# An FFT filter followed by a top-128 FFN on one core: first input in four pieces, inner tables in two, work moved between engines, and an order of issue written out

## The chip, the cores and the metric

The kernel runs on one core of a Trainium2 chip. The core has TensorE (PE in the rows; its weight loads are PEld), VectorE (DVE), ScalarE (ACT) and GpSimd (POOL), and SyncE (SP), which here only issues DMAs. Each engine takes its instructions in the order in which they were issued to it and waits where one of them needs a result that isn't there. The metric is the time of one execution on the device, in microseconds.

## The reference

```python
def _attn_ref(x, filt_r, filt_i):            # x: 8 x 3136 x 256
    X = np.fft.rfft(x, axis=1)
    F = (filt_r + 1j * filt_i)[None, :, :]
    return np.fft.irfft(X * F, n=x.shape[1], axis=1)

def _moe_ref(x, w_gate, w1, w2, capacity):   # capacity 128, w1: 256 x 1024
    scores = np.einsum('bsd,d->bs', x, w_gate)
    out = x.copy()
    for b in range(B):
        top_idx = np.argpartition(-scores[b], capacity)[:capacity]
        xe = x[b, top_idx]
        h = np.maximum(xe @ w1, 0.0)
        g = 1.0 / (1.0 + np.exp(-scores[b, top_idx]))
        out[b, top_idx] = x[b, top_idx] + g[:, None] * (h @ w2)
    return out
```

## The kernel before

The transform over 3136 = 98 x 32 points is done as two short transforms, both as matmuls with tables, for one batch of 8 at a time. A batch goes through these steps, which the code calls by short names:

- `load` brings a batch's half (128 of 256 channels) into the tile `X`, 113 partitions by 4096 values: one DMA for 112 partitions, one for the last row. There is one buffer for each half, so the next batch's half is loaded after the results of an earlier one were stored from it.
- `outer`, in 8 chunks of 32 channels: two `fold`s (sum and difference of the two halves of the points, into `xh` and in place), then four matmuls `amm` (tile `pa`). In the chunks of the list `UNF` ("plain") the folds are left out and `amm` is eight matmuls. `tout` turns the result with a transpose on DVE into `UU`. On the way back `tin` (a transpose into `t`), `ymm` (tile `py`) and `yout` (copy to `X`), and `store`. In the last two batches `imm`, `iout` and two `join`s on DVE or POOL (list `JOIN`) stand in their place.
- `inner`, in 7 groups of two table pairs (the last has one): `zmm` (tile `pz`, with the table `tf_sb`), then the products with the filter: `zout` (ACT copies `pz` to `q`) and `qmul` (POOL multiplies `q` by `fb_sb`), and `pmul` (DVE multiplies `pz` by `fa_sb` into `y`); then `vmm` (tile `pv`, with the table `ti_sb`) over both, and `vout` (ACT copies `pv` back to `UU`). The score of each row comes from `gate` (DVE, one per row group, tile `rj`), or for the pairs listed in `GPOOL` from `gmul` on POOL (tile `xl`, one buffer) and two sums `gsum` on ACT.
- `select` finds the top 128 of a batch by eight counting steps (`count` on ACT, `total` on PE, `over` on DVE or, where `SELM` is 0, on ACT) and some twenty small steps.
- `ffn` gathers the rows, runs the two layers and scatters. The first two batches go alone, then batches 2 to 4 and 5 to 6 together with each factor split in two, and the last batch alone at the end.

At the start there are 85 small matmuls without a purpose for the result (`warmup`), the first `load`, the tables `tf_sb` and `ti_sb` (half of the latter's columns is made on the chip by `turn_ti`: two copies on DVE, two negations on ACT), and the filter tables in four parts (`tables`), which have half of the partitions filled by copies (`spread`).

`z`, `a`, `v`, `y` and `m` are PSUM rings with one buffer each. All steps are put into a list with `op(when, engine, cost, function, reads, writes, ...)`. A planner in the kernel then takes them one by one, by estimated costs and by due times with a lead for each kind of step (the table `LEAN`), and the steps are issued in the order that comes out.

## Time and profile before

| | us |
|---|---|
| median of 3 runs | 492.16 |
| lowest and highest | 490.76, 493.91 |
| the profiled execution | 487.98 |
| its span on the core | 486.2 |
| PE, DVE, ACT, POOL busy | 441.9, 406.4, 288.3, 286.5 |

The span is from the first to the last instruction; 1.8 us of the execution lie around it. The profiled execution is 4.2 us shorter than the median of the other runs. A PE that is busy need not be at its peak, since matmuls overlap and their ends are modelled.

### The profile page before, as it was taken

To read this page: it belongs to the slowest core of one execution; us is meant where nothing else is said; L and a number is where in the kernel's file an instruction comes from. 1 tells how busy PE (TensorE), PEld (TensorE's weight loads), DVE (VectorE), ACT (ScalarE), POOL (GpSimd) and SP (SyncE) were. 2 spreads that over 40 slices of the span, in tenths; PEclk is the share of its full clock that TensorE was granted. 3 is DMA by queue.
4 is the path that set the end of the run, shared out by engine and by line. 5 is a ranking of instruction groups with operands and counts; after the bars stand their busy time and mean duration, and the time that the engine had idled before them with its cause. 6 is when DMAs were issued, how large, how long until landed. Compare 5 with 4: busy or idle time off the path is not lost.

```text
span 486.2 us, 10656 instructions
## 1 busy us (share of the span) xinstructions
PE 441.9 (91%) x4094; PEld 226.1 (47%) x4094; DVE 406.4 (84%) x1012; ACT 288.3 (59%) x603; POOL 286.5 (59%) x186
## 2 busy tenths in 40 slices
PE   9848979999899999899999999999998978798996
PEld 9424443334333444343444344345433546466995
DVE  0777979998999989997999999999997987885632
ACT  1056745667446855866577657655666878865320
POOL 0438965853538784857475538255743987966022
PEclk9978989999999999999999999999999989999999
DMA  8999715137186638462828382818340844534510
GB/s 218 279 244 251 200 45 154 36 93 196 32 242 176 170 95 216 127 182 56 224 58 236 97 229 66 241 44 218 72 134 4 253 135 101 150 72 117 122 45 32
DMA packets 59944, 68.87 MB, mean 142 GB/s; under 512 B 3174, under 2 KB 56422, under 8 KB 57830
## 3 DMA queue, kind: packets, MB, share of 16 engines
q1 hardware_dynamic: 59126, 66.10, 51.0%
q0 software_dynamic: 768, 2.10, 1.3%
q8 instruction: 32, 0.52, 0.5%
q14 instruction: 18, 0.15, 0.1%
HBM read 41.28 MB, written 26.91 MB: 140 GB/s over the span
## 4 chain that ended last, share of the span: by engine, by line
PE 34%; DVE 30%; DMA 19%; ACT 5%; issue 5%; POOL 4%; SPq 1%; POOLq 0%; DVEq 0%; ACTq 0%
PE py L447 8%; PE pv L301 7%; DMA X<-in_x_dram 6%; PE pa L381 6%; DVE UU L386 5%; DVE rj L317 5%; DMA ti_sb<-in_ti_dram 5%; DVE y L289 4%; DVE t L362 4%; DMA out_dram<-X 4%; PE pz L281 3%; DMA fb_sb<-in_fri_dram 3%; DVE X L370 2%; PE pa L410 2%; DVE xh L370 2%
## 5 line engine op out<-in xcount | busy, mean ns | idle before, releaser
L292 POOL TENSOR_TENSOR q<-q,fb_sb 128x1024 f32<-128x1024 f32 (+1 forms) x56 | 126.2, 2253 | 88.2 <-ACT q L285 75.1
L447 PE MATMUL py<-t,c_sb 128*98 128x512 f32 x192 | 104.8, 628 | 4.4 <-ACT X L450 3.9
L381 PE MATMUL pa<-X,c_sb 49*64 49x512 f32 x440 | 79.4, 601 | 2.8 <-DVE UU L386 1.2
L362 DVE STREAM_TRANSPOSE t<-UU 128x1024 f32<-128x1024 f32 x64 | 78.6, 1231 | 1.0 <-PE py L447 0.9
L301 PE MATMUL pv<-y,ti_sb 64*64 64x256 f32 x800 | 68.9, 397 | 8.0 <-DVE rj L317 7.8
L450 ACT COPY X<-py 98x512 f32<-98x512 f32 x96 | 55.7, 581 | 33.9 <-PE py L447 27.2
L317 DVE SCALAR_TENSOR_TENSOR rj<-pv,wg_sb 128x256 bf16<-128x256 f32 x150 | 62.9, 419 | 15.2 <-ACT UU L309 5.3
L386 DVE STREAM_TRANSPOSE UU<-pa 128x1024 f32<-128x1024 f32 x59 | 73.4, 1244 | 2.4 <-PE pa L381 1.5
L281 PE MATMUL pz<-UU,tf_sb 64*64 64x256 f32 x800 | 61.4, 406 | 9.8 <-DVE UU L386 5.0
L289 DVE TENSOR_TENSOR y<-pz,fa_sb 128x1024 f32<-128x1024 f32 (+1 forms) x56 | 63.5, 1134 | 7.5 <-ACT q L285 6.3
L285 ACT COPY q<-pz 128x1024 f32<-128x1024 f32 (+1 forms) x56 | 53.1, 948 | 24.4 <-PE pz L281 23.1
L301 PE MATMUL pv<-q,ti_sb 64*64 64x256 f32 x800 | 66.6, 385 | 0.0
L381 PE MATMUL pa<-xh,c_sb 49*64 49x512 f32 x168 | 50.4, 606 | 4.2 <-DVE UU L386 3.1
L370 POOL TENSOR_TENSOR xh<-X 113x512 f32<-113x512 f32 x27 | 37.4, 1385 | 27.2 <-DMA X<-in_x_dram 19.8
L281 PEld LDWEIGHTS pz<-UU,tf_sb 64*64 64x64 f32 x800 | 27.7, 135 | 49.8 <-issue 14.3
L301 PEld LDWEIGHTS pv<-y,ti_sb 64*64 64x64 f32 x800 | 29.7, 136 | 44.0 <-issue 10.0
L331 POOL TENSOR_TENSOR xl<-UU,wg_sb 128x512 f32<-128x512 f32 x25 | 34.7, 1387 | 15.8 <-ACT UU L311 11.6
L447 PEld LDWEIGHTS py<-t,c_sb 128*98 128x98 f32 x192 | 23.9, 163 | 36.3 <-ACT X L450 17.4
L588 ACT ACTIVATE junk<-R,nb 128x392 bf16<-128x392 f32 (+1 forms) x48 | 30.0, 625 | 18.1 <-DVE nb L607 16.8
L301 PEld LDWEIGHTS pv<-q,ti_sb 64*64 64x64 f32 x800 | 34.4, 137 | 12.9 <-issue 1.0
L309 ACT COPY UU<-pv 128x1024 f32<-128x1024 f32 x24 | 24.3, 1014 | 26.0 <-PE pv L301 25.9
L370 POOL TENSOR_TENSOR X<-X 113x512 f32<-113x512 f32 x23 | 30.6, 1332 | 13.0 <-DVE xh L370 11.9
(201 smaller groups left out, 696.8 us busy)
## 6 DMA issues: line engine op xcount, KB each, us to landing
X<-in_x_dram SPq DMA_DIRECT2D x16, 1792.0 KB
...
```

The lines of the kernel that those rows point to most:

```text
L281: nc.tensor.matmul(z[o, hi, e], lhsT=tf_sb[p, l], rhs=urow(b, l, 0, D)[p], start=True, stop=True)
L285: nc.scalar.copy(out=wide(q), in_=wide(h["z"]))
L289: nc.vector.tensor_tensor(out=wide(y), in0=wide(h["z"]), in1=filt(fa_sb), op=ALU.mult)
L292: nc.gpsimd.tensor_tensor(out=wide(h["q"]), in0=wide(h["q"]), in1=filt(fb_sb), op=ALU.mult)
L301: nc.tensor.matmul(v[o, j, c], lhsT=ti_at[p, k, 2 * i + e, hi], rhs=y[p, hi, c], start=k == 0, stop=k == 1)
L317: nc.vector.scalar_tensor_tensor(out=rj, in0=h["v"][:, k % 2, k // 2 * D:k // 2 * D + D], scalar=1.0, in1=wg_sb, op0=ALU.mult, op1=ALU.mul ...
L362: nc.vector.transpose(out=h["t"].rearrange("p d (l j) -> p d l j", j=2), in_=uchan(b_out, c))
L370: eng.tensor_tensor(out=(area(1) if k else h["f"])[:64 + NH], in0=area(0)[:64 + NH], in1=area(1)[:64 + NH], op=(ALU.add, ALU.subtract)[k])
L381: nc.tensor.matmul(ap[64 * k:64 * k + 64, g].rearrange("p (n d) -> p n d", d=DW), lhsT=todo[k][i][0][p], rhs=todo[k][i][1][p], start=i == ...
L386: nc.vector.transpose(out=uchan(b_in, c), in_=a.rearrange("p (l j) d -> p d l j", j=2))
L447: nc.tensor.matmul(yp[:N1], lhsT=cc["wi"], rhs=half(), start=True, stop=True)
L450: nc.scalar.copy(out=XO[:N1, hx, :, q * CW - hx * HD:(q + 1) * CW - hx * HD], in_=h["y", k][:N1])
```

## The change

1. The planner is gone. A list `ORDER` of 1803 numbers says in which order the steps of the list are issued. The numbers in `PLAN` are others too; the times among them no longer do anything but number the steps.
2. The first batch's input lies in DRAM by quarters of the channels, and is loaded in four pieces of 112 x 2048 values, each with its last row. In all loads that last row is now cut into 16 runs and goes ahead of the rest.
3. `tf_sb` is loaded in two pieces, one for the first two groups and one for the others, and so is `ti_sb`. The work of `turn_ti` is in eight pieces on DVE, ACT and POOL.
4. In the groups of `QDVE` (10 of 56; four of these are the short last group) the second product is made by DVE straight from `pz` (`qdir`), without ACT's copy and POOL's product.
5. `GPOOL` names pairs of either half of a group. 46 pairs go to POOL and ACT, 25 before.
6. There are 17 plain chunks, 20 before. Of the folds 17 are on DVE and 77 on POOL, 38 and 50 before. Where both joins of a chunk are on DVE (three chunks), they read the second operand from PSUM and one copy of ACT's goes.
7. `over` is on ACT in four batches, in two before; on DVE in four, in six before.

```diff
+ORDER = [
+    4, 6, 27, 3, 28, 29, 1, 30, 31, 18, 8, 19, 7, 9, 21, 23, 24, 11, 22, 25, 5, 32, 26, 16, 10, 12, 0, 35, 33, 13, 39,
...
+    QDVE=[[1, 2, 6], [0, 3, 6], [5, 6], [0], [6], [], [], []],
...
-    SELM=[1, 1, 0, 1, 1, 1, 0, 1],
+    SELM=[1, 0, 0, 1, 1, 1, 0, 0],
...
-    UNF=[[3, 4, 5, 7], [0, 3, 4, 6, 7], [0, 4], [0, 2], [], [0, 4], [0, 6, 7], [1, 7]],
-    GPOOL=[[0, 1, 2, 4, 5], [1, 2, 5], [2, 3, 4], [0, 2], [1, 3], [0, 2, 3], [1, 3, 4], [0, 1, 2, 3]],
+    UNF=[[0, 3, 4, 6, 7], [0, 1, 4, 7], [0], [0], [], [0, 4], [0, 6], [1, 7]],
+    GPOOL=[[0, 2, 7, 9, 10], [2, 3, 5, 8, 9, 10, 11], [0, 1, 4, 5, 8, 9, 10], [0, 2, 5, 6, 10, 11], [0, 1, 2, 3, 6,
+          9], [1, 3, 5, 6, 7, 9], [2, 3, 5, 7, 9], [1, 3, 5, 7]],
...
+            def qdir(h=h, wide=wide, filt=filt):
+                h["q"] = q = flt.tile([128, 2, 2 * D], F32, name="q", bufs=BUFS["q"])
+                nc.vector.tensor_tensor(out=wide(q), in0=wide(h["z"]), in1=filt(fb_sb), op=ALU.mult)
...
+            def fetch():
+                nc.sync.dma_start(out=to[112:113].rearrange("p (r e) -> p r e", r=16), in_=ends[h:h + 1])
+                nc.sync.dma_start(out=to[:112], in_=main[h])
...
+        def quarter(q):
+            to = x_flat[:, 2048 * q:2048 * q + 2048]
+            nc.sync.dma_start(out=to[112:113].rearrange("p (r e) -> p r e", r=16), in_=ends[q:q + 1])
+            nc.sync.dma_start(out=to[:112], in_=main[q])
...
+        to, of_ = (ti_sb[re, 1, at], ti_sb[im, 0, at]) if k else (ti_sb[im, 1, at], ti_sb[re, 0, at])
+        if eng == "act":
+            nc.scalar.activation(out=to, in_=of_, func=AF.Copy, scale=-1.0 if k else 1.0)
         else:
-            nc.scalar.activation(out=ti_sb[re, 1], in_=ti_sb[im, 0], func=AF.Copy, scale=-1.0)
+            (nc.vector if eng == "dve" else nc.gpsimd).tensor_scalar(out=to, in0=of_, scalar1=-1.0 if k else 1.0, scalar2=None, op0=ALU.mult)
...
     with tc.manual_schedule():
-        for n in order:
+        for n in ORDER:
             prog[n][4]()
```

In three places the move is shown by the instructions in a row. The first is SP's queue of DMAs at the start of the program, from the first input on; before (`in_x_dram` is the input, `in_fri_dram` the filter, `tf`, `ti` the inner tables):

```order
L475 DMA X<-in_x_dram 112x4096
L476 DMA X<-in_x_dram 1x4096
L991 DMA tf_sb<-in_tf_dram 128x1600
L1018 DMA ti_sb<-in_ti_dram 128x1664
L992 DMA wg_sb<-in_moe_w_gate_dram 128x256
L959 DMA UU<-in_cst_dram 128x16
L943 DMA fa_sb<-in_fri_dram 32x1024 x2
L943 DMA fb_sb<-in_fri_dram 32x1024 x2
```

and now, from the main part of the third quarter that is issued:

```order
L600 DMA X<-in_x_dram 112x2048
L1148 DMA ti_sb<-in_ti_dram 128x512
L1118 DMA tf_sb<-in_tf_dram 128x512
L1085 DMA UU<-in_cst_dram 128x16
L1120 DMA wg_sb<-in_moe_w_gate_dram 128x256
L599 DMA X<-in_x_dram 1x16x128
L600 DMA X<-in_x_dram 112x2048
L1069 DMA fa_sb<-in_fri_dram 32x1024 x2
L1069 DMA fb_sb<-in_fri_dram 32x1024 x2
```

The longer piece of `ti_sb` (128 x 1152) now stands ahead of all input, the short pieces of both tables behind three quarters of it, the fourth quarter behind these, and the longer piece of `tf_sb` behind the third part of the filter.

The second is DVE at the start, the end of the first batch's transposes into `UU` and what follows up to the first product; before (L977 are the copies of `turn_ti`, L950 those of `spread`, L962 fills a constant):

```order
L386 STREAM_TRANSPOSE UU<-pz 128x32x16x2
L977 COPY ti_sb<-ti_sb 32x1664
L386 STREAM_TRANSPOSE UU<-pv 128x32x16x2
L386 STREAM_TRANSPOSE UU<-pa 128x32x16x2
L977 COPY ti_sb<-ti_sb 32x1664
L386 STREAM_TRANSPOSE UU<-pz 128x32x16x2
L962 CAST cr_sb<-UU 128x16
L950 COPY fb_sb<-fb_sb 32x1024
L950 COPY fa_sb<-fa_sb 32x2048
L289 TENSOR_TENSOR y<-pz,fa_sb 128x1024 x2
```

and now:

```order
L488 STREAM_TRANSPOSE UU<-pv 128x32x16x2
L1076 COPY fb_sb<-fb_sb 32x1024
L488 STREAM_TRANSPOSE UU<-pa 128x32x16x2
L1106 TENSOR_SCALAR ti_sb<-ti_sb 32x512
L1088 CAST cr_sb<-UU 128x16
L1076 COPY fb_sb<-fb_sb 32x1024
L488 STREAM_TRANSPOSE UU<-pz 128x32x16x2
L1076 COPY fb_sb<-fb_sb 32x2048
L380 TENSOR_TENSOR y<-pz,fa_sb 128x1024 x2
L387 TENSOR_TENSOR q<-pz,fb_sb 128x1024
```

The long copies of `ti_sb` are no longer among the last transposes; two copies of `fb_sb` are there in their place, and the second group's second product follows the first products on DVE.

The third is POOL while the fifth batch's inner groups run (`q` are the products of `qmul`, `xl` those of `gmul`, `xh` and `X` the folds); before:

```order
L292 TENSOR_TENSOR q<-q,fb_sb 128x1024 x2
L331 TENSOR_TENSOR xl<-UU,wg_sb 128x512
L292 TENSOR_TENSOR q<-q,fb_sb 128x1024
L370 TENSOR_TENSOR xh<-X 113x512
L370 TENSOR_TENSOR X<-X 113x16x32
L292 TENSOR_TENSOR q<-q,fb_sb 128x1024
L370 TENSOR_TENSOR X<-X 113x16x32
L370 TENSOR_TENSOR xh<-X 113x512
L331 TENSOR_TENSOR xl<-UU,wg_sb 128x512
L292 TENSOR_TENSOR q<-q,fb_sb 128x1024
```

and now:

```order
L431 TENSOR_TENSOR xl<-UU,wg_sb 128x512
L472 TENSOR_TENSOR X<-X 113x16x32
L383 TENSOR_TENSOR q<-q,fb_sb 128x1024
L431 TENSOR_TENSOR xl<-UU,wg_sb 128x512
L383 TENSOR_TENSOR q<-q,fb_sb 128x1024 x2
L472 TENSOR_TENSOR X<-X 113x16x32
L472 TENSOR_TENSOR xh<-X 113x512
L431 TENSOR_TENSOR xl<-UU,wg_sb 128x512
L472 TENSOR_TENSOR xh<-X 113x512
L472 TENSOR_TENSOR X<-X 113x16x32
L383 TENSOR_TENSOR q<-q,fb_sb 128x1024
L431 TENSOR_TENSOR xl<-UU,wg_sb 128x512 x3
```

More folds and gate products stand between the products `q` on POOL, and three gate products stand in a row.

## Rows read from the trace of the kernel before

**Rows 1.** By stretch: length; PE, PEld, DVE, ACT, POOL busy; clock, DMA share, GB/s.
```profile
0.00:25.00 25.00, 22.65 (x247) 16.50 (x250) 9.55 (x9) 1.49 (x2) 5.99 (x10) 1.00 0.94 248
25.00:77.00 52.00, 38.49 (x442) 19.52 (x437) 42.95 (x62) 32.22 (x42) 36.76 (x21) 0.87 0.71 183
77.00:370.00 293.00, 280.94 (x2571) 118.03 (x2564) 273.32 (x712) 185.56 (x390) 172.83 (x102) 1.00 0.51 139
370.00:480.00 110.00, 98.30 (x840) 70.74 (x839) 80.12 (x229) 68.99 (x171) 69.99 (x52) 0.98 0.42 112
```
**Rows 2.** Whom PE waited for from 77 to 370 us: total, times, longest.
```profile
PE py L447 <- ACT X L450: 3.2, 6, 1.2
PE pa L381 <- DVE UU L386: 2.3, 5, 0.8
...
PE pv L301 <- DVE nd L593: 0.2, 1, 0.2
```
**Rows 3.** The start in order of time: start, duration, what.
```profile
1.21 0.41 SPq L475 DMA_DIRECT2D X<-in_x_dram  x1
...
12.54 0.69 DVE L370 TENSOR_TENSOR xh<-X 113x512 f32<-113x512 f32 x1 [12.54 <-DMA X<-in_x_dram]
...
20.67 1.28 POOL L370 TENSOR_TENSOR xh<-X 113x512 f32<-113x512 f32 x1 [1.93 <-DMA X<-in_x_dram]
...
25.88 1.02 DVE L977 COPY ti_sb<-ti_sb 32x1664 f32<-32x1664 f32 x1 [0.91 <-DMA ti_sb<-in_ti_dram]
...
29.30 1.02 DVE L977 COPY ti_sb<-ti_sb 32x1664 f32<-32x1664 f32 x1
...
31.66 1.99 PE L281 MATMUL pz<-UU,tf_sb 64*64 64x256 f32 x16 [4.06 <-DVE UU L386]
```
**Rows 4.** The chain that ended last: start, duration, what.
```profile
31.05 13.22 DMA fb_sb<-in_fri_dram
...
152.38 1.02 PE pa L381 x8
...
362.84 1.95 PE pa L381 x16
```
**Rows 5.** Groups of instructions of the gate: busy us, mean ns of one.
```profile
L317 DVE SCALAR_TENSOR_TENSOR rj<-pv,wg_sb 128x256 bf16<-128x256 f32 x150 | 62.9, 419 | 15.2 <-ACT UU L309 5.3 <-ACT UU L305 3.6 <-ACT UU L311 3.3
...
L331 POOL TENSOR_TENSOR xl<-UU,wg_sb 128x512 f32<-128x512 f32 x25 | 34.7, 1387 | 15.8 <-ACT UU L311 11.6 <-ACT Dt L506 2.2 <-ACT UU L309 2.0
...
L336 ACT ACTIVATE junk<-xl 128x256 bf16<-128x256 f32 x50 | 20.9, 418 | 6.5 <-POOL xl L331 5.3 <-ACT junk L588 0.4
...
L317 DVE DVE_READ_ACCUMULATOR rj<-pv,wg_sb 128x1 f32 x150 | 12.3, 82 | 0.0
...
L336 ACT ACTIVATION_READ_ACCUMULATOR junk<-xl 128x1 f32 x50 | 9.5, 189 | 0.0
```
**Rows 6.** Instructions of the folds' line: ns min/median/max, first and last start.
```profile
L370 POOL TENSOR_TENSOR xh<-X x27: 1251/1287/1762, 12.6 to 348.3; 113x512 f32<-113x512 f32 x27
...
L370 DVE TENSOR_TENSOR X<-X x21: 676/1209/2756, 13.3 to 356.2; 113x512 f32<-113x512 f32 x21
L370 DVE TENSOR_TENSOR xh<-X x17: 670/693/1985, 12.5 to 354.3; 113x512 f32<-113x512 f32 x17
```
**Rows 7.** Groups of the products with the filter, as in rows 5.
```profile
L292 POOL TENSOR_TENSOR q<-q,fb_sb 128x1024 f32<-128x1024 f32 x48 | 116.1, 2418 | 71.3 <-ACT q L285 58.2 <-ACT Dt L506 10.0 <-issue 2.0
...
L289 DVE TENSOR_TENSOR y<-pz,fa_sb 128x1024 f32<-128x1024 f32 x48 | 58.1, 1211 | 7.5 <-ACT q L285 6.3 <-issue 1.2
...
L285 ACT COPY q<-pz 128x1024 f32<-128x1024 f32 x48 | 48.5, 1010 | 23.8 <-PE pz L281 22.7 <-POOL q L292 0.6 <-POOL X L419 0.3
```
**Rows 8.** Groups of a counting step's end and of ACT's table load, as in rows 5.
```profile
L607 DVE TENSOR_SCALAR nb<-J,nd 128x1 f32<-128x1 f32 x48 | 10.3, 214 | 1.8
...
L612 ACT ACTIVATE nb<-J,nd 128x1 f32<-128x1 f32 x16 | 4.7, 295 | 0.5
...
L983 ACT ACT_TABLE_LOAD x1 | 1.3, 1283 | 0.7 <-PEq L1161 0.7
```

More of the change, by code (lines that the diff above doesn't have):

```diff
@@ L24 @@
 NROW = 13
+CUT = 2
 W7 = NROW * N2
@@ L320, in inner @@
             parts = sorted({part_of[2 * i + e] for e in range(m)})
-            op(t0, "pe", .49 * m + .04, zmm, [u for l in ls for u in row(b, l)] + ["tf"], new=Z, mode=1)
-            op(t0 + 1.0, "act", .09 + .43 * m, zout, [Z], [Z], new=Q)
+            op(t0, "pe", .49 * m + .04, zmm, [u for l in ls for u in row(b, l)] + [("tf", int(i >= CUT))], new=Z, mode=1)
+            direct = i in QDVE[b]
+            if not direct:
+                op(t0 + 1.0, "act", .09 + .43 * m, zout, [Z], [Z], new=Q)
@@ L323, in inner @@
             op(t0 + 1.0, "dve", .08 + .535 * m, pmul, [Z, *(("fa", k) for k in parts)], new=Y)
-            op(t0 + 2.0, "pool", .1 + 1.13 * m, qmul, [Q, *(("fb", k) for k in parts)], [Q])
-            op(t0 + 4.5, "pe", .88 * m + .02, vmm, [Y, Q, "ti"], new=V, mode=1)
+            if direct:
+                op(t0 + 1.1, "dve", .08 + .535 * m, qdir, [Z, *(("fb", k) for k in parts)], new=Q)
+            else:
+                op(t0 + 2.0, "pool", .1 + 1.13 * m, qmul, [Q, *(("fb", k) for k in parts)], [Q])
@@ L338, in inner @@
-            for ks in ([0, 1], [2, 3]):
-                ks = [k for k in ks if k < n]
-                if i in GPOOL[b] and ks == [2, 3]:
-                    G = ("xl", "g", b, i)
-                    op(t0 + 7.2, "pool", 1.3, gmul, [*(u for l in ls[2:] for u in row(b, l)), "wg"], new=G)
-                    op(t0 + 8.5, "act", .9, gsum, [G], [("u", b % 2, l, NDC) for l in ls[2:]])
+                    nc.scalar.activation(out=rk, in_=h["g", e][:, j], func=AF.Copy, accum_out=urow(b, ls[2 * e + j], D, DS))
@@ L344, in inner @@
+            for e in range(2):
+                ks = [k for k in (2 * e, 2 * e + 1) if k < n]
+                if 2 * i + e in GPOOL[b] and len(ks) == 2:
+                    G, us = ("xl", "g", b, i, e), ls[2 * e:2 * e + 2]
+                    op(t0 + 7.2, "pool", 1.3, lambda e=e, gmul=gmul: gmul(e), [*(u for l in us for u in row(b, l)), "wg"], new=G, tag="gmul")
+                    op(t0 + 8.5, "act", .9, lambda e=e, gsum=gsum: gsum(e), [G], [("u", b % 2, l, NDC) for l in us], tag="gsum")
                     continue
@@ L401, in outer @@
                 continue
-            if b_out >= B - INV:
+            if 2 * b_out + hx in INVH:
                 ir = IRING[c % len(IRING)]
                 PI_, E_ = (ir, "I", b_out, c), ("xh", "i", b_out, c)
+                on_dve = [2 * c + k in JOIN[b_out] for k in range(2)]
+                direct = all(on_dve)
                 def imm(h=h, ir=ir):
@@ L1065 @@
-    bufs = BUFS
-    full = {k: set(v) for k, v in uses.items()}
-    rings = {k: [[None, 0.0] for _ in range(n)] for k, n in bufs.items()}
-    users = [[] for _ in prog]
-    for n, d in enumerate(deps):
-        for m in d:
-            users[m].append(n)
-    left, ready, done = [len(d) for d in deps], [0.0] * len(prog), {}
-    free, can = {p[2]: 0.0 for p in prog}, {p[2]: [] for p in prog}
-    place_of, seen, pemode = {}, {}, 0
-    win, acc, cold = 0, 0.0, 0.0
-    free["sp"] = 1.0
-    for n, p in enumerate(prog):
-        if not left[n]:
-            can[p[2]].append(n)
```

214 lines of the change are left out of this document (80 added, 134 removed), and 85 rows, old and new, of the table ORDER.

## The prediction

> **What bounds the kernel now.** I read the busy times by stretch first, cut where the character of the work changes [rows 1]. From 0 to 25 us the DMA engines are busy for 0.94 of the time and move 248 GB/s: the start is a matter of bytes. From 25 to 77 us, up to the first transposes of the way back, PE is busy for 38.5 of 52 us, at a mean granted clock of 0.87, beside DVE with 43.0; the DMA engines are still at 0.71. From 77 to 370 us six batches pass in 293 us: PE is busy for 280.9 and DVE for 273.3, that is 96% and 93%. POOL (172.8) and ACT (185.6) have a third of that stretch free. The end, 370 to 480 us, has 11.7 us without PE and 29.9 without DVE.
>
> So PE is the bound of the middle, with DVE close behind, and what can be won there without less work on PE is its 12.1 us of idle time. Whom PE waited for there is in the waits [rows 2]: ACT's `yout` with 3.2 us is the first, then eleven rows with DVE as releaser, from 2.3 to 0.2 us, 7.1 us in all, and one of 0.8 for a DMA. This caps the worth of a faster DVE in the middle at 7 us, however much it is relieved.
>
> **The change part by part.** Work on PE: three plain chunks fewer. A plain `amm` took 1.95 us, one on folds 1.02 [rows 4], so 3 x 0.93 = 2.8 us less. PE has no cover for these, so I count them in full, -2.8.
>
> Work on DVE. The gate: 21 pairs, 42 instructions, leave it at 0.419 + 0.082 us each [rows 5]: -21.0. Folds: 14 in place and 7 into `xh` leave, at the medians 1.209 and 0.693 us [rows 6]: -21.8. `qdir`: six full products as long as `pmul`, 1.211 us [rows 7], and four half as large, at about half: +9.7. Three joins more at a fold's 0.693: +2.1. Two batches' eight steps of `over`, two instructions each, the second 0.214 us [rows 8], the first taken as equal: -6.8. Sum -38 us of 406.
>
> Work on POOL. 21 products for the gate at 1.387 [rows 5]: +29.1. 27 folds at 1.287 [rows 6]: +34.7. Six full products at 2.418 [rows 7] and four of half the size leave: -19.3. Three joins leave, at a fold's 1.287: -3.9. Sum +41 us of 286. On ACT: 42 sums at 0.418 + 0.189 [rows 5], +25.5; 16 `over` with two instructions of about 0.295 [rows 8], +9.4; ten copies, four of them half as large, at 1.010 [rows 7], -8.1. Sum +27 of 288. A second table load of 1.28 us (the one of before stood ahead of everything [rows 8]) now comes after the first `zout`. I cost it at nothing, since ACT's next necessary step there, the first `vout`, waits for the first `vmm`; without that cover it is 1.3 us.
>
> What the shift is worth in the middle. Nearly all of the DVE work leaves between 77 and 370 us, since batch 0 and batch 7 keep their number of gate pairs. DVE goes from 93% to about 80% there, POOL from 59% to about 73% and ACT from 63% to about 72%. PE's waits for DVE, 7.1 us, are bounded by none and all of them gone. I take 4 of them as gone, nearer to all, because a transpose or a gate on which PE waits was queued behind other DVE work in a 93% busy queue. Against it I set 1 us for ACT: `yout` is already the longest row of PE's waits [rows 2], and ACT gets sums and counting steps put between. Bounds of that: 0 and 3.2, its doubling. Net -3, with ends -7.1 and +3.2.
>
> Here a rule could speak against the change. The folds on DVE show what two engines do to each other: 0.670 us at best, a median of 1.209 and 2.756 at worst for the same shape [rows 6], and the products on POOL average 2.418. The Trainium skill says (Perfetto Trace Analysis, section Optimizing Scalar/DVE Operations) that DVE and GpSimd share an SBUF read port, so that moving work between the two might not help; by SBUF — State Buffer (section Who interferes with whom) it is DVE instructions with two SBUF inputs that collide. The rows agree as to the folds. But what moves away is folds, which collide, and gates, which read PSUM; the two-input instructions on DVE fall from 49 (38 folds, 11 joins) to 25. So by the rule, too, collisions on DVE would fall; no term rests on it.
>
> The start. Before, the first half of x landed at 12.5 us and the second at 20.7 [rows 3], 1.85 MB in 8.1 us. DVE then held two copies of `ti_sb` of 1.02 us among the last transposes, the first after 0.91 us of waiting for its DMA, and the first `zmm` of batch 0 ran at 31.66 us. Now 0.59 MB of `ti_sb` goes ahead of x, and 0.66 MB of tables, gate weights and constants between the third and the fourth quarter. The fourth quarter is therefore the later one: 1.25 MB more ahead of it, at 248 GB/s [rows 1] 5.0 us, on 20.7 gives 25.7. The last row of each load, a DMA of its own, no longer adds a whole row of 16 KB to one DMA engine beside seven on each; at an eighth of 8.1 us for each of two halves this gives back up to 2.0 us. So x is complete between 23.7 and 25.7 us instead of 20.7. Behind it stand two plain `amm` (the clock may be halved there as it was before), transposes and the two short copies of `fb_sb`: 24 + 2 x 1.95 + 1.2 + 0.7 gives the first `zmm` at about 30 us. That is 1.7 us gained where the bytes say a loss of 3 to 5, because `ti_sb` is then long finished. After that the chain of before waited for the third filter part up to 44.3 us [rows 4]. It is now ahead of the second half of the next x's rows, but the longer piece of `tf_sb`, which the third group needs, stands behind it; that lands at about the same 42 to 44 us. DVE's work from there to the end of batch 0 is unchanged within 1 us (two folds fewer, two products more). I take -2.5 for the stretch up to 77 us: 1.7 from the first `zmm` and something for the last two filter copies, which now come earlier. Ends: -6 (half of PE's 13.5 us of idle time goes) and +2 (the fourth quarter at 25.7 with a halved clock).
>
> The end. PE's idle 11.7 us after 370 us [rows 1] are spread over joins, gathers and the small steps of `select`. The split-weight matmuls now start among the last `imm`, so some of it fills; the last batch's `over` goes to ACT, which makes its counting longer by some 0.3 us in each of eight steps, but it stood some 10 us ahead of its use. I take -2, ends -5 and +2.
>
> Sum: -2.8 - 3 - 2.5 - 2 = -10.3 us. The profiled execution's 487.98 would become 477.7. It is 4.2 us under the median 492.16, so for a median I set the same difference there: **481.9, say 482**.
>
> **The rivals.** (A) The forecast, -10. (B) PE is the bound in any case. Consecutive matmuls into the same single buffer have to wait for its copy whoever is fast: `ymm`, then `yout`, then the next `ymm`, and the new order has such pairs as well. Then DVE's relief gives nothing, the end nothing, and only plain chunks and half of the start remain: -2.8 - 1.2 = -4, 488. For it: the first row of PE's waits is ACT. Against it: 7.1 us of DVE rows. (C) The balance frees more than the waits name, since a wait is put down to the last releaser alone, and the order is made for the new balance: -2.8 - 7.1 - 6 - 2, about -18, 474. For it: between a group's first and second matmuls the new order has more other PE work in batches 4 to 7. (D) Slower: POOL's queue. POOL gets 48 more instructions of about 1.35 us [rows 5, 6] (21 gate products and 27 folds), they stand between the products `q` for which `vmm` waits, and gate products in a row have to wait for two sums on ACT, 1.2 us, as `xl` has one buffer. If one in three of the 48 is ahead of a product that PE needs at once, 16 x 1.35 = 22 us come against 10 won: +11, 503. It decides from about one in six on (8 x 1.35 = 11 us). Against it: POOL sat idle for 71 us ahead of full products [rows 7], nearly all until ACT's copy was there, so it was usually early. (E) The fourth quarter decides the start: +2 there instead of -2.5, and with the rest as in A -6: 486.
>
> **How the numbers follow.** The measurement of this kernel can tell about 1% from no change (three runs of before lay 3.2 us apart). That puts the bounds at 487.2 and 497.1. A has 0.45, from 477 to 487; B 0.20; C 0.14; D 0.11; E 0.10. Faster by over 1%: nearly all of A (0.43), C, a third of B and two thirds of E, 0.70 in all, which I lower to 0.68. Within 1%: 0.20. Slower: D and the worst of E, 0.12. The range leaves out the far ends of C and most of D: 474 to 493.
>
> **What the profile of the changed kernel would show.** From about 75 us on six batches should pass in 286 us or so, with PE at 97% and DVE near 80%; PE's waits should name DVE for 3 us or less and ACT for more. The first `zmm` should stand at 30 us and DVE should reach the first transposes of the way back 2 us earlier. If POOL's products wait for nothing and PE's `vmm` waits for POOL, D was right. If DVE is at 80% and PE at 96% as before, B was. I would be wrong altogether if PE's busy time itself grew, by a halved clock in the middle.

## The result, and the profile after

The changed kernel takes **472.68 us** (median of 4 runs, 470.73 to 474.86), the kernel before 491.84 beside it: ratio 0.9607, interval 0.9553 to 0.9661. That is 19.2 us less where 10 were forecast, and 1.3 us under the lower end of the range. The profiled execution took 470.73 us with a span of 469.0 (before 487.98 and 486.2), so the two traces compared here differ by 17.2 us.

The first view is again the busy time by stretch. I cut where the same work stands as in [rows 1]: 76.3 us is just behind the first transpose of the way back, 356 just behind the seventh batch's `vs`, and 462.8 leaves the same 6.2 us at the end.

```profile
0.00:25.00 25.00, 22.89 (x242) 15.53 (x242) 9.30 (x9) 5.39 (x5) 7.05 (x11) 1.00 0.95 236
25.00:76.30 51.30, 39.66 (x471) 19.05 (x472) 42.00 (x63) 27.82 (x40) 36.99 (x23) 0.90 0.83 203
76.30:356.00 279.70, 270.80 (x2505) 115.94 (x2501) 245.47 (x591) 200.59 (x488) 209.22 (x137) 1.00 0.53 143
356.00:462.80 106.80, 99.33 (x857) 70.96 (x853) 77.58 (x211) 73.55 (x195) 66.13 (x50) 0.98 0.43 115
462.80:469.00 6.20, 1.46 (x11) 1.26 (x11) 0.48 (x1) 0.00 (x0) 0.96 (x1) 0.89 0.12 42
```

Against [rows 1] a stretch's time has two parts, PE busy and PE idle (length less the first figure). Idle: 15.9 to 13.8 us up to the first transposes, 12.1 to 8.9 in the middle, and 16.4 to 12.2 from there to the end (11.7 and 4.7 before, the last from the row 480 to 486.2: 1.52 busy of 6.20). That is -9.5 us. Busy: 441.90 to 434.15, -7.8 us. In the middle DVE went from 93% to 88%, POOL from 59% to 75%, ACT from 63% to 72%.

Whom PE waited for in the middle (total, times, longest), to be read against [rows 2]: ACT is still first, and of the eleven DVE rows (7.1 us) five remain with 4.4 us, 1.7 of them one wait for `vs`.

```profile
PE py L553 <- ACT X L556: 4.1, 7, 0.8
PE pm L627 <- DVE vs L622: 1.7, 1, 1.7
PE pa L483 <- DMA X<-in_x_dram: 1.0, 1, 1.0
PE pz L372 <- DVE q L387: 0.9, 1, 0.9
PE pa L483 <- DVE UU L488: 0.7, 2, 0.5
PE pm L723 <- DVE rows L832: 0.6, 1, 0.6
PE pz L372 <- DVE UU L488: 0.5, 1, 0.5
```

Over the whole span one wait is gone nearly altogether: `vmm` for the gate, which reads the one bank `pv` that the next `vmm` needs. The groups of the first half of `vmm`, before (L301) and after (L396); busy us and mean ns, then PE's idle time ahead of them:

```profile
L301 PE MATMUL pv<-y,ti_sb 64*64 64x256 f32 x800 | 68.9, 397 | 8.0 <-DVE rj L317 7.8 <-DVE nd L593 0.2
```
```profile
L396 PE MATMUL pv<-y,ti_sb 64*64 64x256 f32 x800 | 67.3, 385 | 2.1 <-ACT X L520 1.8 <-DVE rj L412 0.2
```

Of these 7.8 us only 1.3 lay in the middle. The kernel before had the others from 25 to 77 us and from 370 us on:

```profile
PE pv L301 <- DVE rj L317: 3.9, 4, 1.8
PE pv L301 <- DVE rj L317: 2.5, 2, 2.0
```

All rows of PE's waits that name DVE, added up over the whole span, come to 27.9 us before and 16.6 after. So 11.3 us of such waits went, and the middle has 2.7 of them.

The rows that answer to [rows 5 to 7], gate, folds and products, in two views of the changed kernel: groups, and the folds' line with ns min/median/max. A gate's instruction and a product cost what they did; the folds on DVE are fewer and no longer reach 2.76 us.

```profile
L412 DVE SCALAR_TENSOR_TENSOR rj<-pv,wg_sb 128x256 bf16<-128x256 f32 x108 | 45.3, 419 | 10.5 <-ACT UU L404 5.0 <-ACT UU L406 2.0 <-ACT UU L400 1.3
L431 POOL TENSOR_TENSOR xl<-UU,wg_sb 128x512 f32<-128x512 f32 x46 | 62.4, 1358 | 24.2 <-ACT junk L436 19.4 <-ACT UU L406 2.4 <-ACT UU L404 1.5
L383 POOL TENSOR_TENSOR q<-q,fb_sb 128x1024 f32<-128x1024 f32 x42 | 100.3, 2388 | 43.8 <-ACT q L376 43.5 <-DMA X<-in_x_dram 0.3
```
```profile
L472 POOL TENSOR_TENSOR xh<-X x37: 1253/1285/1716, 10.9 to 344.6; 113x512 f32<-113x512 f32 x37
L472 DVE TENSOR_TENSOR xh<-X x10: 649/764/1707, 58.3 to 296.1; 113x512 f32<-113x512 f32 x10
L472 DVE TENSOR_TENSOR X<-X x7: 651/725/1757, 12.2 to 263.6; 113x512 f32<-113x512 f32 x7
```

The start, answering to [rows 3]. The fourth quarter is there at 26.08 us and the last `amm` ends at 29.75, but the first `zmm` stands at 33.77, 2.1 us later than before:

```profile
29.35 0.42 DVE L1106 TENSOR_SCALAR ti_sb<-ti_sb 32x512 f32<-32x512 f32 x1
29.79 1.89 POOL L1076 COPY fa_sb<-fa_sb 32x2048 f32<-32x2048 f32 x1 [2.41 <-DVE ti_sb L1106]
29.80 1.91 DVE L1088 CAST cr_sb<-UU 128x16 fp32r<-128x16 f32 x1
...
32.46 1.25 DVE L488 STREAM_TRANSPOSE UU<-pz 128x1024 f32<-128x1024 f32 x1
...
33.77 1.66 PE L372 MATMUL pz<-UU,tf_sb 64*64 64x256 f32 x16 [4.02 <-DVE UU L488]
```

The list puts the CAST, the copy of `fb_sb` (0.69 us) and only then the last transpose, for which `zmm` waits. The CAST has 16 columns and took 1.91 us, from the start to the end of the copy on POOL beside it. In the kernel before it stood behind that transpose and took

```profile
31.64 0.18 DVE L962 CAST cr_sb<-UU 128x16 fp32r<-128x16 f32 x1
```

### The profile page after: what moved, and what is told of

Its sections match the earlier page's. It is cut to its first block, busy times and chain, and to the rows that moved or that the text cites. A ratio compares the mean times of both kernels' runs of the same rounds, so it can differ in the third digit from the quotient of the medians.

```text
span 469.0 us, 10671 instructions
## 1 busy us (share of the span) xinstructions
PE 434.1 (93%) x4070; PEld 222.8 (47%) x4070; DVE 374.8 (80%) x873; ACT 307.4 (66%) x725; POOL 320.4 (68%) x222
## 4 chain that ended last, share of the span: by engine, by line
PE 47%; DVE 15%; DMA 14%; POOL 9%; ACT 8%; issue 4%; SPq 1%; POOLq 0%; DVEq 0%; ACTq 0%
DMA X<-in_x_dram 12%; PE py L553 11%; PE pv L396 10%; PE pa L483 7%; PE pz L372 6%; DVE UU L488 3%; POOL q L383 3%; DVE y L380 2%; POOL xh L472 2%; POOL xl L431 2%; PE pa L514 2%; DVE t L462 2%; DMA out_dram<-X 2%; DVE rj L412 2%; POOL X L472 2%
## 5 line engine op out<-in xcount | busy, mean ns | idle before, releaser
L383 POOL TENSOR_TENSOR q<-q,fb_sb 128x1024 f32<-128x1024 f32 (+1 forms) x46 | 105.4, 2291 | 45.4 <-ACT q L376 45.1
L431 POOL TENSOR_TENSOR xl<-UU,wg_sb 128x512 f32<-128x512 f32 x46 | 62.4, 1358 | 24.2 <-ACT junk L436 19.4
L396 PE MATMUL pv<-y,ti_sb 64*64 64x256 f32 x800 | 67.3, 385 | 2.1 <-ACT X L520 1.8
L396 PE MATMUL pv<-q,ti_sb 64*64 64x256 f32 x800 | 65.3, 376 | 0.0
L472 POOL TENSOR_TENSOR xh<-X 113x512 f32<-113x512 f32 x37 | 47.9, 1297 | 22.5 <-DMA X<-in_x_dram 17.5
L472 POOL TENSOR_TENSOR X<-X 113x512 f32<-113x512 f32 x40 | 52.3, 1310 | 5.6 <-DVE xh L472 4.2
L376 ACT COPY q<-pz 128x1024 f32<-128x1024 f32 (+1 forms) x46 | 44.6, 970 | 14.2 <-PE pz L372 14.2
L412 DVE SCALAR_TENSOR_TENSOR rj<-pv,wg_sb 128x256 bf16<-128x256 f32 x108 | 45.3, 419 | 10.5 <-ACT UU L404 5.0
L372 PEld LDWEIGHTS pz<-UU,tf_sb 64*64 64x64 f32 x800 | 28.2, 133 | 49.0 <-DVE y L380 12.2
L483 PE MATMUL pa<-xh,c_sb 49*64 49x512 f32 x176 | 49.4, 608 | 1.9 <-DVE UU L488 1.9
L396 PEld LDWEIGHTS pv<-y,ti_sb 64*64 64x64 f32 x800 | 29.6, 133 | 32.6 <-issue 12.5
L436 ACT ACTIVATE junk<-xl 128x256 bf16<-128x256 f32 x92 | 38.4, 417 | 7.3 <-POOL xl L431 5.5
L396 PEld LDWEIGHTS pv<-q,ti_sb 64*64 64x64 f32 x800 | 33.4, 133 | 12.3 <-issue 0.2
```

What stands on the lines that cost most here:

```text
L372: nc.tensor.matmul(z[o, hi, e], lhsT=tf_sb[p, l], rhs=urow(b, l, 0, D)[p], start=True, stop=True)
L383: nc.gpsimd.tensor_tensor(out=wide(h["q"]), in0=wide(h["q"]), in1=filt(fb_sb), op=ALU.mult)
L396: nc.tensor.matmul(v[o, j, c], lhsT=ti_at[p, k, 2 * i + e, hi], rhs=y[p, hi, c], start=k == 0, stop=k == 1)
L412: nc.vector.scalar_tensor_tensor(out=rj, in0=h["v"][:, k % 2, k // 2 * D:k // 2 * D + D], scalar=1.0, in1=wg_sb, op0=ALU.mult, op1=ALU.mul ...
L431: nc.gpsimd.tensor_tensor(out=g, in0=u.rearrange("p d j -> p j d"), in1=wg_sb[:, None, :].to_broadcast([128, 2, D]), op=ALU.mult)
L472: eng.tensor_tensor(out=(area(1) if k else h["f"])[:64 + NH], in0=area(0)[:64 + NH], in1=area(1)[:64 + NH], op=(ALU.add, ALU.subtract)[k])
```

## The experiments

All are measured on the chip; the kernel before ran beside each and gave medians of 489.4 to 491.8 us. "The split" is who does what (`QDVE`, `GPOOL`, `FOLD`, `JOIN`, `UNF`, `SELM`, `SPR`, `WPOOL`), "the list" the order of issue. The rivals: **R**, relieving DVE is the gain; **O**, the new order is the gain whoever does the side work; **J** (later **F**), order and split are worth something only together.

### Order or split alone

```diff
 # order_only: order of issue and loads of after, split of before
-    QDVE=[[1, 2, 6], [0, 3, 6], [5, 6], [0], [6], [], [], []],
+    QDVE=[[], [], [], [], [], [], [], []],
...
-                direct = all(on_dve)
+                direct = False
```


> The changed kernel with the split of work of the kernel before: the same 20 plain chunks, 25 gate pairs on POOL, all 56 products q on POOL, the folds, joins, counting steps and table copies on the engines of before, joins through ACT. Its list is that of after, with each step at the place of the step that it stands for. Theory R (the relief of DVE is the gain): DVE is back at about 400 us of busy time, PE waits for it again, 486 us or more. Theory O (the order of issue is the gain, whoever does the side work): 478 us or less, some 3 us above the changed kernel for the three plain chunks. Theory J (order and split fit each other only): slower than before, over 492 us.

**526.41 us** (521.35 to 531.21). Not merely without gain: every execution was at least 29 us slower than the median of the kernel before, which has the same split.

```diff
 # assign_only: the kernel before, list of before written out, split of after
-    GPOOL=[[0, 1, 2, 4, 5], [1, 2, 5], [2, 3, 4], [0, 2], [1, 3], [0, 2, 3], [1, 3, 4], [0, 1, 2, 3]],
+    GPOOL=[[0, 2, 7, 9, 10], [2, 3, 5, 8, 9, 10, 11], [0, 1, 4, 5, 8, 9, 10], [0, 2, 5, 6, 10, 11], [0, 1, 2, 3, 6,
...
```


> The kernel before, its start and its loads untouched, with the split of work of after (17 plain chunks, 46 gate pairs on POOL, 10 products q on DVE, folds, joins, counting steps and copies on the engines of after). Its order is that of before, each step at the place of the step that it replaces. Theory R: most of the gain is there, 480 us or less. Theory O: only the three plain chunks are gained, 487 to 490 us. Theory J: POOL's longer queue stands in the way of the products in an order not made for it, 492 us or more.

**558.67 us**, ratio 1.1394 (1.1311 to 1.1476). DVE is busy for 378.5 us, nearly as relieved as in the changed kernel (374.8), and nothing is won. The first rows of PE's waits, one of order_only and two of assign_only:

```profile
PE pa L484 <- DVE UU L489: 11.3, 8, 6.4
```
```profile
PE py L553 <- ACT X L556: 22.3, 14, 3.8
PE pm L703 <- ACT junk L694: 9.4, 4, 4.9
```

The work that has moved to ACT (sums, `over`) now stands in ACT's queue ahead of `yout` and of the counting, and PE waits there. Ahead of the longest of these waits, 4.9 us for a `count`, a sum itself waited for POOL's gate product:

```profile
179.87 0.42 ACT L438 ACTIVATE junk<-xl 128x256 bf16<-128x256 f32 x1 [3.73 <-POOL xl L433]
```

Part of the loss is the clock: PE did 31.8 us of its work at 1.2 GHz in order_only and 58.4 in assign_only, 12.5 in the kernel before. Half of that is lost, which makes 10 of the 33 us between the profiled spans of order_only and the kernel before, and 23 of the 64 of assign_only. R and O by themselves fall: J.

### One part put back or taken further, in the list of after

```diff
 # folds_back: folds of chunks that both kernels fold, engines of before
-    FOLD=[[3, 5, 12, 13], [0, 1, 2, 9, 10, 14], [0, 1, 3, 8], [0], ...
+    FOLD=[[3, 12, 13], [0, 1, 2, 4, 5, 9, 10, 11, 14], [0, 1, 3, 6, 7, 8, 11, 12], ...
 # gates_back: 25 pairs on POOL
-    GPOOL=[[0, 2, 7, 9, 10], ...
+    GPOOL=[[1, 3, 5, 9, 11], ...
 # folds_pool: no fold on DVE
-    FOLD=[[3, 5, 12, 13], ...
+    FOLD=[[], [], [], [], [], [], [], []],
 # plain_back
-    UNF=[[0, 3, 4, 6, 7], [0, 1, 4, 7], [0], [0], [], [0, 4], [0, 6], [1, 7]],
+    UNF=[[3, 4, 5, 7], [0, 3, 4, 6, 7], [0, 4], [0, 2], [], [0, 4], [0, 6, 7], [1, 7]],
```


> The changed kernel with the folds of all chunks that are folded in both kernels on the engines of before (26 folds go from POOL to DVE and 7 the other way), in the same order. DVE gets about 19 x 0.9 = 17 us more, some 392 us. Theory R: PE's idle time grows by a third of what left DVE in all, 477 us or more. Theory O: within 2 us of the changed kernel, 471 to 475 us.

**493.44 us**, ratio 1.0073 (1.0032 to 1.0114): 33 folds change their engine, 26 to DVE and 7 away from it, and the whole gain is gone. The list is the changed kernel's. Of the 20.1 us between the two profiled spans, 7.8 are PE's busy time with the same 4070 instructions, and most of that is the clock: 24.5 us of PE's work ran at 1.2 GHz, 10.6 in the changed kernel. The other 12.3 us are idle time.

> The changed kernel with 25 gate pairs on POOL instead of 46, as in the kernel before (42 instructions more on DVE, some 21 us; 29 us less on POOL, 25 less on ACT), each gate soon after the copy of its group, otherwise in the same order. Theory R: 477 us or more. Theory O: within 2 us of the changed kernel, 471 to 475 us.

**484.12 us**, ratio 0.9834 (0.9763 to 0.9905): 11 us are gone. `vmm` waits for the gate again, 5.0 us in seven waits.

> The changed kernel with its last 32 folds on DVE moved to POOL too, in the same order: DVE 25 us less, POOL 40 more. Theory R, if less on DVE is the gain: the same or faster, up to 472 us. Theory F, if the order fits this split alone: slower, 476 to 485 us, though DVE is relieved.

**475.06 us**, ratio 0.9693 (0.9641 to 0.9746). The number in the expectation was wrong: 17 folds were left on DVE, not 32, so DVE lost 14.6 us and POOL gained 18.2. More relief gives nothing: 2.4 us slower, with an interval that overlaps that of the changed kernel, and between the two theories.

> The changed kernel with the 20 plain chunks of before instead of 17 (three of its chunks go from plain to folds, six the other way), otherwise in the same order. By the sum of the prediction 2.8 us, 475.5 us. Theory F: more, since the folds that come and go shift the queues, 478 to 484 us.

**480.15 us**, ratio 0.9803 (0.9751 to 0.9855). By stage: from the first `vs` to the last it takes 324.5 us, 3.0 more than the changed kernel, which is about the term of the sum, though 3.4 us of PE's work ran at 1.2 GHz in it and none in the changed kernel's. The other 4.9 are in the start (first `vs` at 83.5 us, not 78.6), where other chunks are folded and 12.5 us of PE's work, not 7.2, ran at 1.2 GHz.

So in a list that fits one split, 33 small steps of some 1 us on other engines cost 21 us. That speaks for F, but it can't say what a split is worth, because each of these kernels has a list made for another. Hence lists made anew.

### A list for each split

The lists of the next kernels were made by moving single steps earlier or later where no dependence forbids it, and keeping what ended sooner by the costs that the planner of the kernel before has in its code. Only `ORDER` is new, so no diff is shown but for the split.

> The kernel before with its loads, its start and its split of work untouched; only the list in which the steps are issued is another one, made for this split by moving single steps as long as the planner's own costs gave a shorter end. Theory F (an order made for its split is the gain, and the split by itself is worth little): 470 to 478 us, DVE still at 405 us of busy time. Theory R (without the relief of DVE no order does it): 484 us or more, with PE waiting for DVE.

**486.13 us**, ratio 0.9919 (0.9881 to 0.9958): the best that the old split gave here, 3.5 us.

> The kernel order_only (loads and start of after, split of work of before) with a list made for it in the same way, starting from the list of after. Theory F: some 45 us under order_only, 475 to 485 us, since its 526 us were a list that didn't fit. Theory R: 495 us or more.

**491.92 us**, ratio 1.007 (1.003 to 1.011): some 30 us better than order_only, so that its 526 was a list that didn't fit; but no better than the kernel before. Between F and R, nearer to R.

> The control of old_split_new_order and new_start_old_split: the changed kernel with its loads and its split of work, but its list thrown away (steps moved at random until nothing of it was left in place) and another one made from there in the same way as in those two. By the planner's costs its end is level with that of new_start_old_split. Theory R (with the split of before an order meets delays that its costs don't know, folds on DVE beside products on POOL above all, and the new split takes these away): 474 to 481 us, well under the 492 of new_start_old_split. Theory F (any list made for its split is alike, and lists made in this way come out some 12 us longer on the chip): 487 to 494 us.

**478.29 us**, ratio 0.9744 (0.9689 to 0.98). The control holds: lists made alike and level by the costs give 491.9 with the old split and 478.3 with the new one. So the split is worth some 13.6 us, which theory F denied: R, with a list of its own as the condition. Some 3 us of it are the three plain chunks, which are work of PE's and no relief of DVE. The clock doesn't explain it: PE did 22.0 us of its work at 1.2 GHz with the new split and 7.6 with the old one. Lists of the same split lie up to 8.5 us apart, so the size is known no better than that; the best list found for each (486.1 above, 469.8 next) puts it at 16.3. The times of the new split, 469.8 to 478.3, and of the old one, 486.1 to 491.9, don't overlap.

> The changed kernel with its own split and a list made from its own list in the same way; by the planner's costs 1.2 us shorter. A look at what such a search does where it starts from a list that fits: if lists found in this way are honoured by the chip with this split, 470 to 474 us; if the search by itself costs some us on the chip, 476 us or more.

**469.84 us** (468.64 to 475.38), ratio 0.9581 (0.9529 to 0.9633). This is the fastest kernel of the study; its interval overlaps that of the changed kernel, so it beats the kernel before and can't be told from the changed one.

### Which part of the split

```diff
 # gates_back_searched, folds_back_searched: GPOOL, FOLD as in gates_back, folds_back, each with a new list
 # old_split_new_gates: new_start_old_split, and
-    GPOOL=[[1, 3, 5, 9, 11], ...
+    GPOOL=[[0, 2, 7, 9, 10], ...
 # old_split_new_folds: new_start_old_split, with the folds on the engines of after in the chunks that both fold (20 on DVE)
 # no_dve_folds: FOLD as in folds_pool, with a new list
```


> The changed kernel with the gate pairs of before (25 on POOL instead of 46) and a list made for that by moving single steps from the list of gates_back; by the planner's costs it ends within 2 us of the list of after. Theory G (the gate: with more of it on DVE the next group's vmm waits for the bank pv): the chip stays behind the costs, 482 to 487 us, and vmm waits for the gate for 4 us or more. Theory P (folds on DVE beside POOL's products run up to four times as long as counted): 472 to 477 us.

**481.68 us**, ratio 0.9866 (0.9797 to 0.9935): just under G's range, and `vmm` waits for the gate for 3.0 us, not 4; P said 477 at most.

> The changed kernel with the folds of folds_back and a list made for it in the same way; by the planner's costs level with gates_back_searched. Theory P: 482 to 487 us, folds on DVE of 1.2 us in the mean instead of 0.95. Theory G: 472 to 477 us.

**488.30 us**, ratio 0.9984 (0.9952 to 1.0016): P's side, and more than P said. The folds on DVE take 1.26 us in the mean.

> new_start_old_split (491.9 us) with the gate pairs of after (46 on POOL), the rest of its split as before, and a list made for it in the same way. Theory G: 475 to 481 us, most of the 13.6 us between the old and the new split. Theory P: 486 us or more.

**495.39 us**, ratio 1.0145 (1.0078 to 1.0212): G fails, P's 486 or more came.

> new_start_old_split with the folds on the engines of after (as far as the chunks are the same ones), the rest of its split as before, and a list made for it in the same way. Theory P: 475 to 481 us. Theory G: 486 us or more, with vmm waiting for the gate.

**485.88 us**, ratio 0.9943 (0.9897 to 0.9988): P fails by 5 us. `vmm` waits for the gate for 2.4 us. Neither part brings the gain alone.

> The changed kernel with all 94 folds on POOL (none on DVE) and a list made for it by moving single steps from the list of folds_pool, until its end by the planner's costs was level with the changed kernel's. Theory P (what makes the chip stay behind a list's costs is folds on DVE that wait for POOL): no such delays are left, the chip is level with the changed kernel, 469 to 475 us, 12 us and more ahead of folds_back_searched. Rival (POOL with 72% of its time full becomes the hindrance, or the search finds lists that the chip doesn't honour in any case): 478 us or more.

**483.25 us**, ratio 0.9828 (0.9788 to 0.9868). P's number was missed by 8 us. So I looked at where: the stretch from the first `vs` to the last holds nearly the same work in all of these, start and end depend on their own pieces of the list. Before, after, folds_back_searched, no_dve_folds, in this order, columns as in [rows 1]:

```profile
79.30:410.00 330.70, 312.96 (x2925) 135.33 (x2924) 305.45 (x804) 217.82 (x465) 206.18 (x123) 0.99 0.51 139
```
```profile
78.60:400.10 321.50, 307.90 (x2900) 137.32 (x2894) 281.58 (x693) 236.76 (x573) 245.19 (x161) 1.00 0.52 142
```
```profile
77.50:411.90 334.40, 314.01 (x2926) 139.43 (x2919) 305.78 (x710) 238.98 (x574) 230.91 (x146) 1.00 0.50 137
```
```profile
84.70:408.20 323.50, 308.44 (x2901) 137.30 (x2894) 273.04 (x680) 237.85 (x576) 261.46 (x175) 1.00 0.52 143
```

The work differs a little, as the counts of PE's instructions say (2925, 2900, 2926, 2901). The kernel before has 24 more in all for its plain chunks. In folds_back_searched, 24 stand behind the first `vs` that the changed kernel has ahead of it; they are worth about 3 us (PE busy for 61.8 us up to the first `vs`, 64.9 in the changed kernel). So no_dve_folds needs 323.5 us, 10.9 less than folds_back_searched, some 8 of it for the same work, and 2.0 more than the changed kernel. What it lost lies outside: its first `vs` is 6.1 us later than in the changed kernel, and its end is 5.2 us longer, most of it one wait of the last batch's counting:

```profile
PE pz L728 <- ACT junk L719: 4.6, 1, 4.6
```

From the first `vs` to the last, in us, over all kernels with a list of their own:

| gates / folds | rest of the split new | rest old |
|---|---|---|
| new / new (or none on DVE) | 321.5, 320.1, 325.0; 323.5 | |
| old / new | 328.3 | 331.3 |
| new / old | 334.4 | 333.5 |
| old / old | | 330.7 (before), 331.5, 336.1 |

(320.1 is after_polished, 325.0 new_split_searched.) With the rest new, old gates cost 3 to 8 us and old folds 9 to 14. For the folds this stands: 9.4 us against the 325.0, whose list was made in the same way and has about as many PE instructions there (2919). For the gates it doesn't: 6.2 us of PE's work in the 328.3 ran at 1.2 GHz (391.3 to 398.1 us), and without the 3.1 that this costs 0 to 5 remain. With the rest old, which has the plain chunks' 3 us in all rows, either part alone wins 3 to 5 against the 336.1 and nothing against 330.7 and 331.5. What lists made in this way scatter by start and end (some 5 us each) is not explained by the split, and I leave it open.

Why a fold on DVE is dear shows in folds_back_searched at 172 us:

```profile
172.75 2.35 POOL L388 TENSOR_TENSOR q<-q,fb_sb 128x1024 f32<-128x1024 f32 x1
172.83 2.82 DVE L477 TENSOR_TENSOR X<-X 113x512 f32<-113x512 f32 x1 [0.50 <-POOL xh L477]
175.06 1.71 POOL L477 TENSOR_TENSOR xh<-X 113x512 f32<-113x512 f32 x1
...
175.71 0.64 PE L488 MATMUL pa<-X,c_sb 49*64 49x512 f32 x1 [1.00 <-DVE X L477]
```

The fold starts 0.08 us after POOL's product, is done 0.55 us after the product's end, and POOL's next fold, 1.28 in the median, then takes 1.71. A fold alone takes 0.65. So the two take turns here, each for a whole instruction; the fold's price is what is left of POOL's instruction, and PE waited 1.00 us for this one. The folds of this kernel come to 45.3 us (19 in place at 1.396, 17 into `xh` at 1.104 in the mean), those of the changed kernel to 16.2. In old_split_new_gates, with the old folds beside more gate products on POOL, they reach 1.548 and 1.200, 1.202 and 1.092 in new_start_old_split. The Trainium skill (SBUF — State Buffer, section Who interferes with whom) states an exclusive lock on the ports that DVE and GpSimd share, and that a `tensor_tensor` of DVE with two SBUF inputs contends there with GpSimd's reads; that whoever issues first holds the ports for the whole instruction, it says of DVE's 2-port modes. These rows agree, and have a whole instruction for a `tensor_tensor` as well.

That these turns are what the folds cost in all isn't shown. The slower folds of old_split_new_gates didn't lengthen its stretch (333.5 us against 336.1), and in after_polished, the fastest, the 17 folds take 1.25 us in the mean. A rival is DVE's load as such: in the stretch it is busy for 305.8 us in folds_back_searched, 281.6 in the changed kernel and 273.0 in no_dve_folds. No run parts the two.

### The start

```diff
 # cast_late, in ORDER (17 is the CAST, 51 the copy of fb_sb, 47 the last transpose)
-    ... 15, 17, 51, 47, ...
+    ... 15, 47, 51, 17, ...
 # filled_start, filled_less: steps put in behind the last amm and the first zmm
+        for _ in range(n):          # n = 60 and 36, then 32 and 18
+            nc.tensor.matmul(wt[:64, :64], lhsT=zeros, rhs=zeros, start=True, stop=True)
```


> The changed kernel with two small DVE steps of the start moved: the 16-column CAST into cr_sb (1.91 us in the changed kernel, 0.18 before) and the first short copy of fb_sb stand behind the last transpose of batch 0 instead of ahead of it. Theory S (the CAST ran as long as the copy on POOL beside it and held up the transpose for which the first zmm waits): CAST back at 0.2 us or off the path, first zmm at 31.2 us instead of 33.8, and up to 2.5 us gained at the end, 470 to 472 us. Rival: the start has slack behind it (the third filter part, the next x), first zmm earlier, but 472.7 us as before.

**472.90 us**, ratio 0.9653 (0.9588 to 0.9718): no gain. The CAST takes 0.17 us, and the first `zmm` waits for 1.41 us behind the last `amm`, not 4.02, as theory S had it. But it stands at 34.24, since that `amm` ended at 32.83 and not at 29.75: the fourth quarter came at 27.47 us, 1.4 later, and the clock was at its lower level (0.51 in the row, that is 1.2 GHz) from 28.3 to 31.8 us, while PE was busy throughout. POOL's copy now meets the `tensor_scalar` that fills part of `ti_sb`, which takes 1.25 us instead of 0.42; it was done 0.08 us behind the `amm`, so that it cost next to nothing:

```profile
28.30:31.80 3.50, 3.50 (x21) 1.34 (x17) 2.12 (x3) 1.88 (x1) 1.57 (x2) 0.51 1.00 264
```
```profile
27.47 2.88 PE L489 MATMUL pa<-X,c_sb 49*64 49x512 f32 x16 [0.95 <-DMA X<-in_x_dram]
30.05 2.78 PE L489 MATMUL pz<-X,c_sb 49*64 49x512 f32 x16
30.74 1.89 POOL L1082 COPY fa_sb<-fa_sb 32x2048 f32<-32x2048 f32 x1 [1.93 <-DMA fa_sb<-in_fri_dram]
31.66 1.25 DVE L1112 TENSOR_SCALAR ti_sb<-ti_sb 32x512 f32<-32x512 f32 x1
...
34.24 1.14 PE L378 MATMUL pz<-UU,tf_sb 64*64 64x256 f32 x16 [1.41 <-DVE UU L494]
```

So the CAST did hold up the first `zmm`; what the start would give without it at the same clock was not seen. The same section of the Trainium skill names `cast`, `copy` and `tensor_scalar` among the DVE operations that can take the shared ports, when their operands meet its conditions; the CAST of the changed kernel and this TENSOR_SCALAR agree.

> The changed kernel with 60 of the warm-up's small matmuls more between the last amm of batch 0 and the first zmm, and 36 more between the first and the second zmm, where PE is idle for 4.0 and 2.4 us. Theory C (the half clock of 34 to 44 us costs what its instructions lose, zmm 1.66 and 1.99 instead of 1.07 us, amm 3.69 instead of 1.95): full clock there, 2 to 3 us gained, 470 us. Rival: the stretch waits for the filter tables in any case, full clock but the same time within 1 us.

**478.16 us**, ratio 0.9757 (0.9701 to 0.9813). A mis-sized experiment: each of the small matmuls is two instructions, the first filling took 7.2 us, and the first `zmm` was pushed to 40.0 us.

> filled_start with about half as many small matmuls (32 and 18, 64 and 36 instructions of some 0.06 us), so that they end before the first and the second zmm are ready. Theory C: full clock from 34 to 44 us, 2 to 3 us gained over the changed kernel, 470 us. Rival: full clock, but the stretch waits for DVE and the tables, 472 to 473 us.

**476.59 us**, ratio 0.9729 (0.968 to 0.9778). Theory C fails here: the granted clock was at its lower level (0.50, that is 1.2 GHz) at other times, ahead of the filling (PE had been busy for 11.1 of the 14.2 us before) and again late in batch 0:

```profile
27.20:30.60 3.40, 3.40 (x20) 1.29 (x19) 0.74 (x1) 0.44 (x1) 1.03 (x1) 0.50 1.01 243
30.60:64.70 34.10, 28.12 (x399) 17.06 (x396) 28.44 (x35) 20.86 (x27) 24.52 (x15) 1.00 1.00 224
64.70:71.50 6.80, 6.49 (x60) 2.88 (x55) 4.61 (x9) 2.48 (x2) 5.84 (x4) 0.50 0.30 83
```

The 34 to 44 us of the expectation ran at full clock, and 3.9 us were lost all the same. One execution had a mean granted clock of 0.997 (0.976 to 0.984 in the changed kernel) and took 474.28 us, so that a higher clock alone didn't bring a gain. What decides where the clock falls stays open.

## Why the prediction was wrong

**The step that failed** is how the relief was priced: PE's waits for DVE were counted in the middle alone ("This caps the worth of a faster DVE in the middle at 7 us, however much it is relieved"), and PE's busy time was changed by the three plain chunks and by nothing else. In the middle the term was right: -3.2 us where -3 was set. But over the whole span the waits that name DVE fell by 11.3 us, of which the middle has 2.7, and PE's busy time fell by 7.8, not 2.8. By the traces the sum is -7.8 - 3.2 - 2.1 - 4.2, some -17, against -2.8 - 3 - 2.5 - 2. Of the 7 us between them 5.0 are PE's busy time and 2.2 the end.

The cap also takes a wait for the whole price, and the folds at their median. The range of a fold was in [rows 6] (0.676 to 2.756 us), and the working named the shared ports and said that "no term rests on it". Between the changed kernel and folds_back_searched the stretch from the first `vs` to the last grows by 12.9 us: about 3 are the work that lies elsewhere, 6.8 are PE's idle time (6.0 of it in rows that name DVE), and another 3 are PE's busy time, which no row of waits has. The rule weighed there, from the Trainium skill (Perfetto Trace Analysis, section Optimizing Scalar/DVE Operations), that moving work from DVE to GpSimd might not help, is not borne out: with all folds on POOL that stretch is some 8 us shorter for the same work than with 36 on DVE.

**Work on PE**, -2.8: measured -7.8. The 24 instructions of three plain chunks are gone as foretold, and in plain_back the middle gives 3.0 us for them. Another 0.9 is the clock. Stretches at 1.2 GHz, before and after, with PE busy for 12.5 and 10.6 us in them, half of which is lost:

```profile
30.00:40.20 10.20, 6.09 (x56) 3.29 (x60) 5.81 (x7) 5.05 (x5) 4.24 (x2) 0.50 0.98 245
64.10:67.60 3.50, 2.98 (x29) 1.99 (x33) 2.67 (x4) 0.00 (x0) 2.82 (x3) 0.51 0.02 5
391.80:395.20 3.40, 3.40 (x28) 1.59 (x20) 2.92 (x5) 2.03 (x5) 3.40 (x3) 0.50 0.00 0
```
```profile
34.20:44.40 10.20, 7.22 (x56) 2.45 (x48) 4.58 (x5) 4.39 (x4) 6.11 (x4) 0.50 0.99 231
423.30:426.70 3.40, 3.40 (x19) 1.87 (x15) 1.82 (x8) 1.68 (x6) 2.28 (x2) 0.50 0.85 217
```

The remaining 4 us are not a faster `vmm`: its mean fell from 397 to 385 ns in the groups above because 7.3 us of it ran at 1.2 GHz before and 0.5 after, and from 95 to 370 us the same group takes 386 and 385. They are put at nothing in the prediction. In folds_back_searched most of them are back: the same 4070 instructions as in the changed kernel, as much of PE's work at 1.2 GHz (10.7 and 10.6 us), and PE busy for 437.6 us, 3.5 more. So a busy PE holds some waiting too. This is one pair of lists, and the cause stays open.

**The middle's idle time**, -3: measured -3.2, with DVE's rows down by 2.7 and ACT's up by 0.9, where 4 and 1 were set. Six batches took 279.7 us, not 286; the difference is PE's work there, part of which the new list does earlier or later (66 instructions fewer in the stretch).

**The start**, -2.5: measured -0.7 (first transposes of the way back at 76.08, before 76.78). The last quarter is there at 26.08, a little behind the bounds of 23.7 to 25.7 and 2.1 behind the 24 that the sum used. That and the CAST, counted at nothing, 1.9 us, put the first `zmm` at 33.8 instead of 30. Idle time up to the first transposes still fell by 2.1 us, later in batch 0, where the waits for the gate, 3.9 us, are gone. No run shows why: batch 0 has as many gate pairs on DVE as before.

**The end**, -2: idle 4.2 us less. It is mis-sized. The waits for the gate give 2.3 of it. From the last `vs` to the end the changed kernel needs 68.9 us and the kernel before 76.2, with 430 and 470 PE instructions and 7.5 and 10.7 us without PE. The list alone doesn't fill that idle time: new_start_old_split, with the old split and a list descended from the new one, needs 69.6 us there with 414 instructions, but has 11.2 us without PE. What filled it stays open.

**The engines' sums**, DVE -38, POOL +41, ACT +27: measured -31.6, +33.9, +19.1, right in sign and order.

**The rivals.** C's number (-18) came near, but not by its terms, which is luck: it had 7.1 us for the middle's waits and 6 for the start, where 3.2 and 2.1 were measured. Its idea, "The balance frees more than the waits name", has PE's busy time for it. B fell: `yout` stayed the first row and the gain came. D's mechanism is there when list and split don't fit (assign_only), through ACT, whose sums wait for POOL's gate products; in the changed kernel POOL's products still had 43.8 us of idle time ahead of them, nearly all until ACT's copy was there. E's later `zmm` was true and didn't decide.
